# The first sequence's 47-point transform kept in its input tile and regrouped by transfers between partitions

## The chip, the cores and the metric

The kernel runs on one core of a Trainium2 chip. The metric is the device time of one execution in microseconds (us). The five engines are named as in the profile: PE (TensorE, matrix products), PEld (its weight loads), DVE (VectorE), ACT (ScalarE), POOL (GpSimd) and SP (SyncE, which here only issues transfers). SPq, ACTq and POOLq are the three queues from which transfers are issued.

## The reference

The input x holds 8 sequences of 3008 positions by 256 channels. Each sequence is transformed, mixed, shrunk and transformed back, and the result goes through a gated two-layer network.

```
X = rfft(x, axis=1)
Yr = soft(Xr @ w_r - Xi @ w_i + b_r, 0.01);  Yi = soft(Xr @ w_i + Xi @ w_r + b_i, 0.01)
y = irfft(Yr + 1j * Yi, n=3008, axis=1)
out = (sigmoid(y @ w_gate) * (y @ w_val)) @ w_out        # 256 -> 1536 -> 256
```

Here soft(v, l) = sign(v) * max(|v| - l, 0). The network's weights come in as 64-bit floats and are turned into pairs of shorter floats on the chip ("conversion").

## The kernel before

3008 = 47 * 64. The transform of a sequence runs in two steps. Step A (`fwd_a`, L176) is a 47-point transform along the partitions: 94 input partitions hold 47 positions for each half j of the 64, a table `fa_sb` has 96 columns, and the 96 outputs are 24 frequencies k by four rows (real or imaginary part, half j). A sequence has 32 columns of 256 channels; `load_a` (L165) brings four columns at a time as two transfers (64 and 30 partitions), so h runs from 0 to 7. `fwd_a` makes two products of 512 columns per h, and ACT and DVE copy the results from PSUM back over the input tile, in place. `half_a` (L192) is the same for two columns at a time and is used for the third group of sequences (called `beside`).

Step B (`fwd_b`, L226) is a 64-point transform for two frequencies at a time, so a sequence has 12 steps q. It needs the 64 positions of a frequency, real and imaginary, on 128 partitions. So the outputs of step A are regrouped: `store_a` (L183) writes them to `zd` in DRAM, and `load_b` (L221) reads `zd` back into the tile `zf` with another arrangement of partitions. For the first sequence, step q then does `fwd_b(0, q)`, `mix4(0, q-1)` (the mixing, 24 products) and `inv_b(0, q-2)` (the inverse 64-point transform, 4 products), whose result `vz` goes to `vd` in DRAM. Later `load_v` (L313) reads `vd` and `inv_a` (L329) makes the inverse 47-point transform, whose output is the network's input. `load_mf` and `load_mi` bring the tables of each step, two buffers each.

The order at the beginning is written out by hand (L827 to L896, `manual_schedule`): all loads of the first sequence; its step A with the stores on SP, and four loads of the second sequence between them; tables and biases; step A of the second sequence for h = 0 to 3 with the stores on POOL; then the loop over q = 0 to 13 with the first sequence's steps and, beside them, conversion of the first weights (`load_part`, `start_part`, `ops`); then step A of the second sequence for h = 4 to 7. Behind it the first chunk of the network runs, 12 units `ffn[f]`: `ffn1` makes 12 products of 512 columns, conversion of the next weights hangs in its gaps (`hook`), and after each unit come five or six `half_a`. What is not in a manual block is placed by the planner where an engine has room; that is how two loads of the table `mis` and their copies to `md` (L216, L217, on POOL) come to stand near the end of the loop. Before anything, `WARM` = 24 products of zeros run on PE (L817). Each engine and each queue works in the order in which it is given its instructions, so a waiting transfer holds those behind it on its queue.

The lines the change touches are the step A helpers (L146 to L197), `load_b` (L221), the fused biases (L744), `load_part` and `start_part` (L786, L795) and the manual order (L815 to L896).

Of the kernel before, what the change touches and what calls it, by code (L numbers as in the profile page):

```python
# [20 lines left out]
NK2 = 24  # L21
# [13 lines left out]
PRE = 2  # L35
WARM = 24
EARLY = 8
NCONV = 7
# [23 lines left out]


def _tables(seq):
    n2 = np.arange(R2)
    k2 = np.arange(NK2)
    c, s = _cs(n2[:, None] * k2[None, :], R2)
    fa = np.zeros((R2, 2, NK2, 2, 2))
    fb = np.zeros((NK2, 2, 2, 128))
    for j in range(2):  # L70
        fa[:, j, :, 0, j] = c
        fa[:, j, :, 1, j] = -s
        fb[:, 0, j, j:2 * R2:2] = c.T / seq
        fb[:, 1, j, j:2 * R2:2] = -s.T / seq
    fa = fa.reshape(2 * R2, 2 * NQ)
    fb = fb.reshape(2 * NQ, 128).astype(np.float32)
# [27 lines left out]
    return {"mf": mf, "mi": mi, "mis": mis, "fa": fa.astype(np.float32), "fb": fb}  # L104


@with_exitstack
def tile_fft_mix_ffn(ctx: ExitStack, tc, x, w_r, w_i, b_r, b_i, w_one, w_out, mf, mi, mis, fa, fb, out):
    nc = tc.nc
# [36 lines left out]
    fa_sb = cw.tile([2 * R2, 2 * NQ], F32, name="fa_sb")  # L146
    nc.scalar.dma_start(fa_sb, fa)

# [16 lines left out]
    def load_a(b, h):  # L165
        xf = p0.tile([P, 4, D], F32, name="xf0", bufs=R1 // 8) if b == 0 else big("xf")
        for lo_, hi_ in ((0, 64), (64, 2 * R2)):
            nc.sync.dma_start(xf[lo_:hi_], xv[b, lo_:hi_, 4 * h:4 * h + 4])
        held["x", b, h] = xf

    def product_a(xi, az, copy):
        pa = bank("pa")[:2 * NQ]
        nc.tensor.matmul(pa, fa_sb, xi, start=True, stop=True)  # L173
        copy(az, pa.rearrange("p (h c) -> p h c", h=2))  # L174

    def fwd_a(b, h):  # L176

        xf = held["x", b, h]
        for i in range(2):
            at = slice(2 * i, 2 * i + 2)  # L180
            product_a(xf[:2 * R2, at], xf[:2 * NQ, at], nc.vector.tensor_copy if b < 2 and i else nc.scalar.copy)

# [3 lines left out]
    def load_half(b, h):  # L186
        xf = p2.tile([P, 2, D], F32, tag="ld", bufs=NLD, name="xfh")
        for lo_, hi_ in ((0, 64), (64, 2 * R2)):
            nc.sync.dma_start(xf[lo_:hi_], xv[b, lo_:hi_, 2 * h:2 * h + 2])
        held["xh", b, h] = xf  # L190
# [30 lines left out]
    def load_b(b, q):  # L221
        zf = p2.tile([P, 2, D], F32, tag="ld", bufs=NLD, name="zf")
        nc.sync.dma_start(zf, zd[b][4 * q:4 * q + 4].rearrange("(q a) n c -> (a n) q c", q=2))
        held["z", b, q] = zf

    def fwd_b(b, q, m, full):  # L226
# [141 lines left out]
    def converting(place):  # L368

        if place == 0:  # L370
            ops("hi", 0)
            n = len(started)
            start_part(p2)
# [53 lines left out]

    def fft_units(bs):

        aa = [(b, h) for b in bs for h in range(R1 // 8)]  # L430
        ms = {}
        units = []
# [10 lines left out]
        def loads(q, b):  # L443
            if b == bs[0]:
                if q == 0:
                    ms[0, 0] = load_mf(0)
                if q + 1 < NP:
                    ms[q + 1, 0] = load_mf(q + 1)
                if 0 <= q - 1 < NP:
                    ms[q - 1, 1] = load_mi(q - 1, False)  # L450
# [287 lines left out]
    def load_mix():  # L738
        for w in (w_r, w_i):
            wf = f2k("wf")  # L740
            nc.sync.dma_start(wf, w.rearrange("(t p) d -> p t d", p=P))
            wfs.append(wf)

    def load_bias():  # L744
        for i, v in enumerate((b_r, b_i)):
            nc.sync.dma_start(bias_sb[:, i], v.rearrange("(o d) -> o d", o=1).broadcast_to([P, D]))
            nc.sync.dma_start(bias4[64 * i:64 * i + 64], v.rearrange("(o d) -> o d", o=1).broadcast_to([64, D]))

    def mix_weights():
        wi = p0.tile([P, CT, 2, D], F32R, tag="xf0", bufs=R1 // 8, name="wi_sb")  # L750
        nc.scalar.copy(wi[:, :, 0], wfs[1])
# [7 lines left out]
        sub(bias_sb[:, 1], bias_sb[:, 1], bias_sb[:, 0])  # L759
        return wi  # L760
# [25 lines left out]
    def load_part():  # L786
        k, f = parts.pop(0)
        if len(parts) >= 3 * NF // 2 - NCONV:
            raw = p0.tile([P, 2, D, 2], U32, tag="xf0", bufs=R1 // 8, name="raw0")
# [5 lines left out]
    def start_part(pool):  # L795
        if not raws:
            return
        k, f, raw = raws.pop(0)
        e = pool.tile([P, 2, D], U32, tag="f2k", bufs=NF2K if pool is p2 else 2, name="cv_e")
        if k:  # L800
# [17 lines left out]
    for _ in range(WARM):  # L818
        nc.tensor.matmul(warm, zero[:, :P], zero, start=True, stop=True)
    second_fft = fft_units(groups[1])[1]  # L820
    third_fft = fft_units(groups[2])[1]
    ffn, own0, u0 = ffn_units()
    na = R1 // 8
    early = EARLY // 2
    nc.vector.memset(ebias, -896.0 * 2.0 ** 23)
    mfs, mis_ = {}, {}
    with tc.manual_schedule():  # L827
        for h in range(na):
            load_a(0, h)
        load_mix()  # L830
        for h in range(na):
            fwd_a(0, h)
            store_a(0, h, nc.sync)
            if 0 <= h - 2 < early:
                load_a(1, h - 2)
        mfs[0] = load_mf(0)
        load_bias()
        for q in range(2):
            load_b(0, q)
        mfs[1] = load_mf(1)  # L840
        for h in range(early):
            fwd_a(1, h)
            store_a(1, h, nc.gpsimd)
            if h == 1:
                wi_sb = mix_weights()
        nc.sync.dma_start(fb_sb, fb)
        for _ in range(2):
            load_part()
        for q in range(NP + 2):
            if q + 2 < NP:  # L850
                load_b(0, q + 2)
            if 0 <= q - 1 < NP:
                mis_[q - 1] = load_mi(q - 1, True)
            if len(parts) > 3 * NF // 2 - NCONV and q % 2 or q == NP:
                load_part()
            if q % 2 == 0 and 4 <= q < 4 + 2 * (na - early):
                load_a(1, early + q // 2 - 2)
            if q < NP:
# [4 lines left out]
            if q % 2:  # L863
                ops("sum word", 0)
                start_part(p0)
                ops("exp low top", -1)
            elif q:
                ops("power mant", -1)
                if len(started) > 1:
                    ops("hi lo", 0)  # L870
                ops("one", -1)
            if 0 <= q - 1 < NP:
                mix4(0, q - 1)
            if 0 <= q - 2 < NP:
                inv_b(0, q - 2, mis_[q - 2], True)
        beside = [(b, h) for b in groups[2] for h in range(R1 // 4)]
        for bh in beside[:2]:
            load_half(*bh)
        left = ["hi lo", "power mant one", "sum word", "hi lo"]
        for h in range(early, na):  # L880
            fwd_a(1, h)
            store_a(1, h, nc.gpsimd)
            ops(left.pop(0), 0)
    p0s.close()
    p3 = p3s.enter_context(tc.tile_pool(name="p3", bufs=2, side="right", reuse_waits="tile"))
    with tc.manual_schedule():
        for u in own0:
            load_v(u)
        for f in range(NF):
            ffn[f]()  # L890
            for i in range(f * len(beside) // NF, (f + 1) * len(beside) // NF):
                if i + 2 < len(beside):
                    load_half(*beside[i + 2])
                half_a(*beside[i])
            if parts:
                load_part()  # L896
    hook.clear()

# [18 lines left out]

    (a3, q3), (a4, q4) = (fft_units(g) for g in groups[3:])
    n = len(a3) // 3
# [112 lines left out]
```

## Time and profile before

| what | value |
|---|---|
| median of 3 runs (lowest, highest) | 2847.21 us (2844.71, 2848.36) |
| profiled execution, its own time | 2847.25 us |
| its span | 2845.1 us |
| PE busy in the span | 2810.8 us (99%) |
| PEld, DVE, ACT, POOL busy | 2315.3, 2082.7, 1320.1, 713.6 us |
| PE busy in the first 220 us | 199.15 us, granted clock 0.95 |
| PE busy in the other 2625 us | 2611.69 us, granted clock 1.00 |
| moved by DMA in the first 220 us | 235 GB/s, engines' mean busy share 0.76 |

The span runs from the first to the last instruction of the profiled execution. A busy share is the part of a stretch in which the engine worked, and the granted clock is 1.00 at 2.4 GHz and 0.50 at 1.2 GHz.

### The profile page before, as it was taken

Reading aid. Unit: us, or ns where it says so; the run is one execution under the profiler, and the core shown is the slowest. Engines: PE = TensorE matmul, PEld = TensorE weight load, DVE = VectorE, ACT = ScalarE, POOL = GpSimd, SP = SyncE. Lnnn points to the kernel's source line nnn. Section 1 sums busy time; section 2 is a strip of 40 time slices with the busy share of each in tenths; the row PEclk is TensorE's granted clock in tenths of the full one; section 3 lists DMA queues with packets and bytes.
Section 4 is the critical chain, followed back from the end, with each engine's and each line's share of the span. In section 5 each row is a group of like instructions: output and inputs, shape, how many; then the busy total and the mean of one; then the engine's idle time right before and its main releaser. Section 6 shows DMA issues by size and latency. Waiting matters only on the chain.

```text
span 2845.1 us, 38347 instructions
## 1 busy us (share of the span) xinstructions
PE 2810.8 (99%) x13892; PEld 2315.3 (81%) x13892; DVE 2082.7 (73%) x3109; ACT 1320.1 (46%) x2294; POOL 713.6 (25%) x642
## 2 busy tenths in 40 slices
PE   8899999999999999999999999999999999999999
PEld 6668888888899987888888888888888888888887
DVE  5668778767678635777777777777777777777776
ACT  4565544555445443444444444444444444444443
POOL 0111001113300001333333333333333333333321
PEclk9999999999999999999999999999999999999999
DMA  8676645666544472000000000000000000000000
GB/s 274 199 237 191 180 136 157 182 181 198 176 144 147 155 207 69 20 11 30 30 30 16 15 30 30 18 13 30 30 30 15 16 30 31 19 11 30 30 16 15
DMA packets 174510, 240.49 MB, mean 85 GB/s; under 512 B 15793, under 2 KB 126097, under 8 KB 174321
## 3 DMA queue, kind: packets, MB, share of 16 engines
q1 hardware_dynamic: 164368, 212.84, 24.4%
q0 software_dynamic: 9856, 25.17, 2.7%
q8 instruction: 110, 1.80, 0.3%
q14 instruction: 80, 0.65, 0.1%
q10 hardware_dynamic: 96, 0.04, 0.0%
HBM read 133.65 MB, written 104.33 MB: 84 GB/s over the span
## 4 chain that ended last, share of the span: by engine, by line
PE 91%; DMA 3%; DVE 3%; issue 2%; ACT 1%; SPq 0%; POOL 0%; DVEq 0%; POOLq 0%; ACTq 0%
PE pd L645 11%; PE pc L645 11%; PE pa L645 11%; PE po L622 8%; PE po L621 8%; PE po L620 7%; PE pm L265 5%; PE pb L645 5%; PE pia L334 4%; PE pb L231 3%; PE pa L173 2%; PE pg L390 2%; PE pg L392 2%; PE pg L391 2%; PE po L415 2%; PE po L416 2%
## 5 line engine op out<-in xcount | busy, mean ns | idle before, releaser
L622 PE MATMUL po<-hl,w 128*128 128x512 f32 x912 | 362.9, 398 | 0.0
L621 PE MATMUL po<-hh,w 128*128 128x512 f32 x912 | 362.0, 397 | 0.0
L620 PE MATMUL po<-hh,w 128*128 128x512 f32 x912 | 361.0, 396 | 0.0
L704 POOL TENSOR_TENSOR c<-c,c 128x512 f32<-128x512 f32 x114 | 147.4, 1293 | 834.5 <-DVE c L700 633.5
L645 PE MATMUL pc<-s,w1h 128*128 128x512 f32 x912 | 284.2, 393 | 1.4 <-DVE v L679 1.4
L645 PE MATMUL pa<-a,w1h 128*128 128x512 f32 x912 | 284.2, 393 | 0.0
L700 DVE TENSOR_TENSOR c<-u,pc 128x512 f32<-128x512 f32 x228 | 156.7, 687 | 115.7 <-PE pc L645 107.4
L675 DVE TENSOR_TENSOR u<-u,pb 128x512 f32<-128x512 f32 x228 | 155.3, 681 | 91.0 <-PE pb L645 64.7
L592 ACT CAST hh<-v 128x512 fp32r<-128x512 f32 x114 | 70.7, 620 | 305.6 <-DVE v L685 305.6
L622 PEld LDWEIGHTS po<-hl,w 128*128 128x128 f32 x912 | 171.6, 188 | 41.8
L620 PEld LDWEIGHTS po<-hh,w 128*128 128x128 f32 x912 | 172.2, 189 | 40.8
L621 PEld LDWEIGHTS po<-hh,w 128*128 128x128 f32 x912 | 171.2, 188 | 40.5
L645 PEld LDWEIGHTS pa<-a,w1h 128*128 128x128 f32 x912 | 171.3, 188 | 40.0
L645 PEld LDWEIGHTS pc<-s,w1h 128*128 128x128 f32 x912 | 171.0, 188 | 39.5 <-DVE v L679 2.3
L596 POOL TENSOR_TENSOR hl<-c,hh 128x512 fp32r<-128x512 f32 x114 | 152.5, 1338 | 186.2 <-ACT hh L592 186.2
L265 PE MATMUL pm<-w_sb,xsh 128*128 128x256 f32 x1008 | 190.4, 289 | 1.5 <-ACT xf L174 1.1
L645 PE MATMUL pc<-s,w1l 128*128 128x512 f32 x456 | 177.7, 390 | 0.0
L645 PE MATMUL pa<-a,w1l 128*128 128x512 f32 x456 | 177.1, 388 | 0.0
L677 DVE TENSOR_TENSOR v<-u,pd 128x512 f32<-128x512 f32 x228 | 156.8, 688 | 24.6 <-PE pd L645 0.6
L706 DVE TENSOR_TENSOR u<-u,pd 128x512 f32<-128x512 f32 x228 | 156.9, 688 | 24.4 <-DVE c L700 0.9
L679 DVE TENSOR_TENSOR v<-v,pc 128x512 f32<-128x512 f32 x228 | 156.6, 687 | 24.4 <-DVE v L677 0.9
L671 ACT COPY u<-pa 128x512 f32<-128x512 f32 x228 | 133.7, 586 | 81.8 <-PE pa L645 81.8
(165 smaller groups left out, 6769.7 us busy)
## 6 DMA issues: line engine op xcount, KB each, us to landing
zf<-zd SPq DMA_DIRECT2D x96, 256.0 KB, 3.5
vf<-vd SPq DMA_DIRECT2D x128, 192.0 KB, 3.2
out_dram<-ot SPq DMA_DIRECT2D x93, 256.0 KB, 2.2
vd<-vz SPq DMA_DIRECT2D x84, 256.0 KB, 2.8
ypair<-yd SPq DMA_DIRECT2D x19, 1024.0 KB, 4.9
yd<-yf SPq DMA_DIRECT2D x103, 188.0 KB, 2.9
zd<-xf SPq DMA_DIRECT2D x40, 384.0 KB, 3.4
xf<-in_x_dram SPq DMA_DIRECT2D x48, 256.0 KB, 4.3
```

What stands on the lines that cost most here:

```text
L265: nc.tensor.matmul(o, l, r, start=(i == 0), stop=(i == len(mms) - 1))
L596: sub_(hl, h, hh)
L620: nc.tensor.matmul(o, wh, hh, start=(f == 0), stop=False)
L621: nc.tensor.matmul(o, wl, hh, start=False, stop=False)
L622: nc.tensor.matmul(o, wh, hl, start=False, stop=(f == NF - 1))
L645: nc.tensor.matmul(o, l, r, start=not more and l is wh and r is xh, stop=l is wl, skip_group_check=more)
L675: add(u, u, b)
L677: add(v, u, d)
L679: add(v, v, c)
L700: add(c12, u, c)
L704: nc.gpsimd.tensor_mul(c12, g12, c12)
L706: add(u, u, d)
```

## The change

The first sequence gets a single tile `xz` of 32 columns instead of eight tiles. Its step A uses a table `fa0` whose columns stand in another order, so that frequency k's four output rows lie at partitions `_row(k)`, +4, +8 and +12. They are not stored to DRAM. `load_b0(q)` builds `zf` by eight transfers within the chip, each from one partition of `xz` (32 KB in a row) to 32 partitions of `zf` (1 KB each): four on SP for the step's first frequency, four on POOL for the second. `store_a` and `load_b` stay for the other sequences.

Around it the order changes. `WARM` is 13. Two h of the second sequence's step A (not four) come before the loop; h = 2 and 3 run in the loop at q = 2 and 4, ahead of `fwd_b`, h = 4 at q = 13 ahead of the last `inv_b`, and h = 5 to 7 after the loop. The stores of h = 0 to 3 go from POOL to SP. The biases for the first sequence are loaded by `load_bias4` before the loop, the other biases and `fb_sb` at q = 3. Weight parts are loaded at even q into three buffers of their own. The tiles of `half_a` come from `r2k` (four buffers) instead of `ld` (three). Three `half_a` run before the first unit of the network, and the next weight part is loaded right behind them. The two `mis` tables are loaded by hand at f = 2 and 3.

```diff
-WARM = 24
-EARLY = 8
+WARM = 13
+EARLY = 2
+AT_FIRST = 3
...
+def _row(k):
+    return k // 8 * 32 + k % 2 * 16 + k % 8 // 2
...
+    for k in range(NK2):
+        fa0[:, _row(k):_row(k) + 16:4] = fa[:, 4 * k:4 * k + 4]
...
+    xz = p0.tile([P, R1 // 2, D], F32, name="xz")
...
     def load_a(b, h):
-        xf = p0.tile([P, 4, D], F32, name="xf0", bufs=R1 // 8) if b == 0 else big("xf")
+        xf = big("xf") if b else xz[:, 4 * h:4 * h + 4]
...
     def load_half(b, h):
-        xf = p2.tile([P, 2, D], F32, tag="ld", bufs=NLD, name="xfh")
+        xf = r2k("xfh").bitcast(F32)
...
+    def load_b0(q):
+        zf = p2.tile([P, 2, D], F32, tag="ld", bufs=NLD, name="zf")
+        for w in range(4):
+            for i in range(2):
+                at = _row(2 * q + i) + 4 * w
+                (nc.gpsimd if i else nc.sync).dma_start(zf[32 * w:32 * w + 32, i], xz[at:at + 1])
+        held["z", 0, q] = zf
...
     with tc.manual_schedule():
         for h in range(na):
             load_a(0, h)
+        nc.sync.dma_start(fa_sb, fa)
+        load_a(1, 0)
         load_mix()
+        load_a(1, 1)
         for h in range(na):
             fwd_a(0, h)
-            store_a(0, h, nc.sync)
-            if 0 <= h - 2 < early:
-                load_a(1, h - 2)
         mfs[0] = load_mf(0)
-        load_bias()
         for q in range(2):
-            load_b(0, q)
+            load_b0(q)
+        load_bias4()
         mfs[1] = load_mf(1)
-        for h in range(early):
+        for h in range(EARLY):
             fwd_a(1, h)
-            store_a(1, h, nc.gpsimd)
-            if h == 1:
+            load_a(1, EARLY + h)
+            if h == 0:
                 wi_sb = mix_weights()
-        nc.sync.dma_start(fb_sb, fb)
-        for _ in range(2):
-            load_part()
         for q in range(NP + 2):
             if q + 2 < NP:
-                load_b(0, q + 2)
+                load_b0(q + 2)
             if 0 <= q - 1 < NP:
                 mis_[q - 1] = load_mi(q - 1, True)
-            if len(parts) > 3 * NF // 2 - NCONV and q % 2 or q == NP:
+            if q < EARLY:
+                store_a(1, q)
+            elif q < 4 + EARLY and q % 2 == 0:
+                h = EARLY + q // 2 - 1
+                fwd_a(1, h)
+                store_a(1, h)
+            if q == 3:
+                nc.sync.dma_start(fb_sb, fb)
+                load_bias()
+            if q % 2 == 0 and q <= NP:
                 load_part()
...
+            if q == NP + 1:
+                fwd_a(1, 2 * EARLY)
+                store_a(1, 2 * EARLY, nc.gpsimd)
             if 0 <= q - 2 < NP:
                 inv_b(0, q - 2, mis_[q - 2], True)
-        for bh in beside[:2]:
+        for bh in beside[:NR2K]:
             load_half(*bh)
...
         for u in own0:
             load_v(u)
+        halves(AT_FIRST)
+        load_part()
         for f in range(NF):
             ffn[f]()
-            for i in range(f * len(beside) // NF, (f + 1) * len(beside) // NF):
-                if i + 2 < len(beside):
-                    load_half(*beside[i + 2])
-                half_a(*beside[i])
             if parts:
                 load_part()
+            if f in (2, 3):
+                tables[f - 2, 1] = load_mi(f - 2, False)
+            halves(AT_FIRST + (f + 1) * (len(beside) - AT_FIRST) // NF)
```

`halves(n)` runs `half_a` up to the n-th and issues, behind each, the load that is four further on.

## Rows read from the trace of the kernel before

**Rows 1.** Windows: stretch, length, busy us (instructions) of PE PEld DVE ACT POOL, clock, DMA, GB/s

```profile
220.00:2845.00 2625.00, 2611.69 (x12954) 2171.02 (x12952) 1947.54 (x2878) 1197.68 (x2074) 681.25 (x582) 1.00 0.23 72
```

**Rows 2.** Waits of PE, first 220 us: us in total, times, longest

```profile
PE pb L231 <- DMA zf<-zd: 7.0, 1, 7.0
PE pia L334 <- DMA vf<-vd: 4.5, 1, 4.5
PE pa L173 <- ACT cv_e L770: 2.6, 1, 2.6
...
PE pb L231 <- DMA mf_sb<-in_mf_dram: 1.3, 1, 1.3
PE pi L299 <- ACT vz L306: 1.2, 1, 1.2
PE pa L173 <- DMA xf<-in_x_dram: 1.0, 3, 0.5
```

**Rows 3.** PE in order of time: start, us, engine, line, operation, shape, count

```profile
1.46 7.10 PE L819 MATMUL warm<-zero 128*128 128x512 f32 x24 [1.46 <-DVE ebias L825]
...
38.13 3.76 PE L231 MATMUL pb<-mf_sb,zf 128*128 128x128 f32 x16 [6.99 <-DMA zf<-zd]
...
50.71 1.05 PE L231 MATMUL pb<-mf_sb,zf 128*128 128x128 f32 x8
...
98.05 7.56 PE L173 MATMUL pa<-xf,fa_sb 94*96 94x512 f32 x16
...
110.07 5.34 PE L334 MATMUL pia<-fb_sb,vf 96*128 96x94 f32 x24 [4.46 <-DMA vf<-vd]
...
117.39 0.63 PE L390 MATMUL pg<-yth,w1h 128*128 128x512 f32 x1
117.81 0.63 PE L391 MATMUL pg<-ytl,w1h 128*128 128x512 f32 x1
...
123.03 0.39 PE L392 MATMUL pg<-yth,w1l 128*128 128x512 f32 x1
123.26 0.39 PE L390 MATMUL pg<-yth,w1h 128*128 128x512 f32 x1
```

**Rows 4.** Windows of the first loads, of step B's begin, of the loop, and of 110 to 120

```profile
4.00:16.00 12.00, 12.00 (x37) 6.35 (x37) 2.43 (x4) 3.61 (x5) 0.00 (x0) 1.00 1.03 248
38.00:42.00 4.00, 3.87 (x18) 3.90 (x19) 0.72 (x2) 1.44 (x4) 0.96 (x2) 0.52 1.04 404
...
50.00:92.00 42.00, 42.00 (x330) 40.98 (x328) 37.16 (x64) 29.49 (x55) 6.48 (x9) 1.00 0.80 239
...
110.00:120.00 10.00, 9.45 (x34) 8.29 (x35) 3.00 (x6) 4.96 (x9) 0.00 (x0) 0.51 0.30 102
```

**Rows 5.** Transfers by issue: count, KB each, us to landing; 0 to 1.2, 300 to 900, 30 to 33

```profile
xf<-in_x_dram SPq DMA_DIRECT2D x1, 256.0 KB, 3.6
...
zf<-zd SPq DMA_DIRECT2D x64, 256.0 KB, 3.3
...
mf_sb<-in_mf_dram SPq DMA_DIRECT2D x32, 128.0 KB, 2.5
...
zf<-zd SPq DMA_DIRECT2D x2, 256.0 KB, 7.5
```

**Rows 6.** SP's queue in order of time: start, us of issuing, transfer, count

```profile
0.74 9.57 SPq L168 DMA_DIRECT2D xf<-in_x_dram  x16
...
104.80 10.95 SPq L317 DMA_DIRECT2D vf<-vd  x4
```

**Rows 7.** DVE in order of time, the last two copies of step A

```profile
20.77 0.69 DVE L174 COPY xf<-pa 96x512 f32<-96x512 f32 x1 [1.03 <-PE pa L173]
22.49 0.69 DVE L174 COPY xf<-pa 96x512 f32<-96x512 f32 x1 [1.03 <-PE pa L173]
```

**Rows 8.** POOL in order of time, around the last result of the loop

```profile
100.92 0.71 POOL L217 DMA_DIRECT2D md<-mi_sb  x1 [1.69 <-DMA mi_sb<-in_mis_dram]
101.63 0.72 POOL L307 DMA_DIRECT2D vd<-vz  x1
```

More of the change, by code (lines that the diff above doesn't have):

```diff
@@ L75, in _tables @@
     fa = fa.reshape(2 * R2, 2 * NQ)
+    fa0 = np.zeros_like(fa)
+    for k in range(NK2):
+        fa0[:, _row(k):_row(k) + 16:4] = fa[:, 4 * k:4 * k + 4]
+    fa0 = fa0.astype(np.float32)
     fb = fb.reshape(2 * NQ, 128).astype(np.float32)
@@ L103, in _tables, with tile_fft_mix_ffn @@
         mis[q, :, 0], mis[q, :, 1] = _split(e.reshape(128, 128))
-    return {"mf": mf, "mi": mi, "mis": mis, "fa": fa.astype(np.float32), "fb": fb}
+    return {"mf": mf, "mi": mi, "mis": mis, "fa0": fa0, "fa": fa.astype(np.float32), "fb": fb}
 @with_exitstack
-def tile_fft_mix_ffn(ctx: ExitStack, tc, x, w_r, w_i, b_r, b_i, w_one, w_out, mf, mi, mis, fa, fb, out):
+def tile_fft_mix_ffn(ctx: ExitStack, tc, x, w_r, w_i, b_r, b_i, w_one, w_out, mf, mi, mis, fa0, fa, fb, out):
     nc = tc.nc
@@ L146, in tile_fft_mix_ffn @@
     fa_sb = cw.tile([2 * R2, 2 * NQ], F32, name="fa_sb")
-    nc.scalar.dma_start(fa_sb, fa)
+    fa0_sb = p0.tile([2 * R2, 2 * NQ], F32, name="fa0_sb")
+    nc.scalar.dma_start(fa0_sb, fa0)
+    xz = p0.tile([P, R1 // 2, D], F32, name="xz")
     zd = [tc.dram_tile([NQ, R1, D], F32, name=f"zd{b}") for b in range(B)]
@@ L169, in load_a, with product_a @@
         held["x", b, h] = xf
-    def product_a(xi, az, copy):
+    def product_a(xi, az, copy, table=fa_sb):
         pa = bank("pa")[:2 * NQ]
-        nc.tensor.matmul(pa, fa_sb, xi, start=True, stop=True)
+        nc.tensor.matmul(pa, table, xi, start=True, stop=True)
         copy(az, pa.rearrange("p (h c) -> p h c", h=2))
@@ L180, in fwd_a @@
             at = slice(2 * i, 2 * i + 2)
-            product_a(xf[:2 * R2, at], xf[:2 * NQ, at], nc.vector.tensor_copy if b < 2 and i else nc.scalar.copy)
+            product_a(xf[:2 * R2, at], xf[:2 * NQ, at], nc.vector.tensor_copy if b < 2 and i else nc.scalar.copy,
+                      fa_sb if b else fa0_sb)
     def store_a(b, h, queue=nc.sync):
@@ L372, in converting @@
             n = len(started)
-            start_part(p2)
+            start_part()
             if len(started) > n:
@@ L425, in ffn2, with fft_units @@
                 nc.sync.dma_start(out[ct * P:(ct + 1) * P, c * CW:(c + 1) * CW], ot)
-    def fft_units(bs):
+    def fft_units(bs, ms):
         aa = [(b, h) for b in bs for h in range(R1 // 8)]
-        ms = {}
         units = []
@@ L448, in loads @@
                     ms[q + 1, 0] = load_mf(q + 1)
-                if 0 <= q - 1 < NP:
+                if 0 <= q - 1 < NP and (q - 1, 1) not in ms:
                     ms[q - 1, 1] = load_mi(q - 1, False)
@@ L742, in load_mix, with load_bias4 @@
             wfs.append(wf)
+    def load_bias4():
+        for i, v in enumerate((b_r, b_i)):
+            nc.sync.dma_start(bias4[64 * i:64 * i + 64], v.rearrange("(o d) -> o d", o=1).broadcast_to([64, D]))
     def load_bias():
@@ L746, in load_bias @@
             nc.sync.dma_start(bias_sb[:, i], v.rearrange("(o d) -> o d", o=1).broadcast_to([P, D]))
-            nc.sync.dma_start(bias4[64 * i:64 * i + 64], v.rearrange("(o d) -> o d", o=1).broadcast_to([64, D]))
     def mix_weights():
-        wi = p0.tile([P, CT, 2, D], F32R, tag="xf0", bufs=R1 // 8, name="wi_sb")
+        wi = p0.tile([P, CT, 2, D], F32R, name="wi_sb")
         nc.scalar.copy(wi[:, :, 0], wfs[1])
@@ L758, in mix_weights @@
             sub(w_sb[:, :, 1, i], w, w_sb[:, :, 0, i])
-        sub(bias_sb[:, 1], bias_sb[:, 1], bias_sb[:, 0])
         return wi
@@ L788, in load_part @@
         if len(parts) >= 3 * NF // 2 - NCONV:
-            raw = p0.tile([P, 2, D, 2], U32, tag="xf0", bufs=R1 // 8, name="raw0")
+            raw = p0.tile([P, 2, D, 2], U32, name="raw0", bufs=3)
         else:
@@ L793, in load_part, with start_part @@
         raws.append((k, f, raw))
-    def start_part(pool):
+    def start_part():
         if not raws:
@@ L798, in start_part @@
         k, f, raw = raws.pop(0)
-        e = pool.tile([P, 2, D], U32, tag="f2k", bufs=NF2K if pool is p2 else 2, name="cv_e")
+        e = p2.tile([P, 2, D], U32, tag="f2k", bufs=NF2K, name="cv_e")
         if k:
@@ L819, in tile_fft_mix_ffn, with halves @@
         nc.tensor.matmul(warm, zero[:, :P], zero, start=True, stop=True)
-    second_fft = fft_units(groups[1])[1]
-    third_fft = fft_units(groups[2])[1]
+    tables = {}
+    second_fft = fft_units(groups[1], tables)[1]
+    third_fft = fft_units(groups[2], {})[1]
     ffn, own0, u0 = ffn_units()
     na = R1 // 8
-    early = EARLY // 2
     nc.vector.memset(ebias, -896.0 * 2.0 ** 23)
     mfs, mis_ = {}, {}
+    beside = [(b, h) for b in groups[2] for h in range(R1 // 4)]
+    waiting = list(beside)
+    def halves(upto):
+        while waiting:
+            i = len(beside) - len(waiting)
+            if i >= upto:
+                break
+            half_a(*waiting.pop(0))
+            if i + NR2K < len(beside):
+                load_half(*beside[i + NR2K])
     with tc.manual_schedule():
@@ L829, in tile_fft_mix_ffn @@
             load_a(0, h)
+        nc.sync.dma_start(fa_sb, fa)
+        load_a(1, 0)
         load_mix()
+        load_a(1, 1)
         for h in range(na):
             fwd_a(0, h)
-            store_a(0, h, nc.sync)
-            if 0 <= h - 2 < early:
-                load_a(1, h - 2)
         mfs[0] = load_mf(0)
-        load_bias()
         for q in range(2):
-            load_b(0, q)
+            load_b0(q)
+        load_bias4()
         mfs[1] = load_mf(1)
-        for h in range(early):
+        for h in range(EARLY):
             fwd_a(1, h)
-            store_a(1, h, nc.gpsimd)
-            if h == 1:
+            load_a(1, EARLY + h)
+            if h == 0:
                 wi_sb = mix_weights()
-        nc.sync.dma_start(fb_sb, fb)
-        for _ in range(2):
-            load_part()
         for q in range(NP + 2):
             if q + 2 < NP:
-                load_b(0, q + 2)
+                load_b0(q + 2)
             if 0 <= q - 1 < NP:
                 mis_[q - 1] = load_mi(q - 1, True)
-            if len(parts) > 3 * NF // 2 - NCONV and q % 2 or q == NP:
+            if q < EARLY:
[8 more added lines that the diff above has]
+            if q % 2 == 0 and q <= NP:
                 load_part()
-            if q % 2 == 0 and 4 <= q < 4 + 2 * (na - early):
-                load_a(1, early + q // 2 - 2)
+            if q % 2 == 0 and 4 <= q < 4 + 2 * (na - 2 * EARLY):
+                load_a(1, 2 * EARLY + q // 2 - 2)
             if q < NP:
@@ L864, in tile_fft_mix_ffn @@
                 ops("sum word", 0)
-                start_part(p0)
+                start_part()
                 ops("exp low top", -1)
@@ L871, in tile_fft_mix_ffn @@
                 ops("one", -1)
+            if q == 4:
+                sub(bias_sb[:, 1], bias_sb[:, 1], bias_sb[:, 0])
             if 0 <= q - 1 < NP:
                 mix4(0, q - 1)
+            if q == NP + 1:
+                fwd_a(1, 2 * EARLY)
+                store_a(1, 2 * EARLY, nc.gpsimd)
             if 0 <= q - 2 < NP:
                 inv_b(0, q - 2, mis_[q - 2], True)
-        beside = [(b, h) for b in groups[2] for h in range(R1 // 4)]
-        for bh in beside[:2]:
+        for bh in beside[:NR2K]:
             load_half(*bh)
         left = ["hi lo", "power mant one", "sum word", "hi lo"]
-        for h in range(early, na):
+        for h in range(2 * EARLY + 1, na):
+            ops(left.pop(0), 0)
             fwd_a(1, h)
             store_a(1, h, nc.gpsimd)
-            ops(left.pop(0), 0)
+        ops(left.pop(0), 0)
     p0s.close()
@@ L916, in merge @@
                                          enumerate(streams) for i, u in enumerate(s)), key=lambda t: t[:2])]
-    (a3, q3), (a4, q4) = (fft_units(g) for g in groups[3:])
+    (a3, q3), (a4, q4) = (fft_units(g, {}) for g in groups[3:])
     n = len(a3) // 3
```

## The prediction

> **What bounds the kernel now.** I read the windows first, because the change touches only the beginning. From 220 us on PE is busy 2611.69 of 2625 us at clock 1.00 [rows 1]: that part is bound by PE, its work stays as it is, and what the beginning wins or loses should reach the end in full. In the first 220 us the list of PE's waits is the next view [rows 2]. It names where PE stood: 7.0 us for the regrouped tile zf, 4.5 for vf (the result read back from DRAM), 2.6 for a conversion on ACT, 1.3 for a table mf, 1.2 for vz, 1.0 for the second sequence's x. Third comes PE in order of time [rows 3]: it shows stretches at half the clock behind two of the waits. The 16 products from 38.13 take 3.76 us where eight take 1.05 later. From 110.07 the 24 inverse products take 5.34, and the network's products follow each other every 0.42 us (117.39, 117.81) against 0.23 (123.03, 123.26). The granted clock was 0.52 from 38 to 42 and 0.51 from 110 to 120 [rows 4], behind 7.0 and 4.5 us in which PE had nothing to do. So the stakes are some 18 us of waits, about 8 us of slow clock, and the zeros at the start.
>
> **The change part by part**, against the profiled execution's own 2847.25 us (span 2845.1), which is the median of the runs (2847.21) but for 0.04.
>
> *Zeros.* Eleven of 24 go. They are the last and ran at the full clock: 11 x 0.23 = 2.5 us. PE is then ready near 6.0. The first x transfer lands 0.74 + 3.6 = 4.3 [rows 5, 6], its second half about 0.6 later, so the data is there. Later h come every 385 KB / 248 GB/s = 1.55 us [rows 4] and are used every 1.72 [rows 7], so no wait follows. **-2.5**; nothing if x came at 8.4.
>
> *Second sequence's x.* Its three waits (1.0) fall on h = 1 to 3, of which two now run in the loop, 10 us after their load. **-1.0.**
>
> *The regrouping.* The last copy of step A ended at 22.49 + 0.69 = 23.2 [rows 7], so now at 20.7. DRAM's round trip from there to 38.13 was 15 us. Now SP issues four transfers and POOL four beside it. SP's x loads took 9.57 / 16 = 0.6 us each to issue [rows 6], POOL's 0.7 [rows 8]; at 0.6 the fourth goes out at 22.5. How long 32 KB from one partition takes, no row shows. From below, at 404 GB/s [rows 4], it is 0.1 us behind the landing time; from above, if the rate goes by partitions, the loads to 94 partitions give 248 / 94 = 2.6 GB/s and 12 us. I take the landing of an undisturbed zf, 3.3 us [rows 5], because a set of eight moves the same 256 KB into the same tile: 25.8. PE finishes its four early products at 23.1 (20 products of 0.86 from 6.0) and waits 2.7.
>
> Behind these four, SP issues the next four, two biases and only then mf(1): seven more of 0.6, so it leaves at 26.7 and lands 2.5 later [rows 5], at 29.2. PE has done the first fwd_b by 26.7 and waits 2.5 again. mf(2) stands behind four x loads, four transfers of the next set, a store and a weight part, leaves near 32.7 and lands at 35.2. PE meanwhile has fwd_b(1) (0.9), mix4(0) (2.8, a step of 4.6 less 0.9 each for fwd_b and inv_b) and the moved step A of h = 2 (1.7), to 34.7: 0.5 left of the 1.3 before. In all 5.7 for 8.3; issues at 0.4 would make it 4. I take **-3.0**, with bounds -6 and +3 (a landing of 7.5, as zf had at 30 us [rows 5]). The slow products at 38.13 cost 3.76 - 2 x 1.05 = 1.6; as PE's waits are now split I keep half: **-0.8**.
>
> *The loop.* A step is 36 instructions; 330 in 42 us [rows 4] make 9.2 steps, 4.6 us each, with PE full. The moved products of the second sequence are the same work elsewhere, cost nothing, and at q = 13 they fill the 1.2 us wait for vz: **-1.2**. Per step SP now issues four transfers, mf, mi and on average one more, 7 x 0.6 = 4.2 us of 4.6; POOL four and vd, 3.5. Both queues just keep up. zf has three buffers, so a set is issued over two steps ahead (9 us): this cover hides a slow landing, though not a low rate. On SP, store_a(1, 2) waits for its copies, with a weight part and mf(4) behind it; mf is needed a step later. The 3 MB that zd took each way on DRAM are gone, and the engines' share in the loop was 0.80. For the extra waits at each fwd_b I put **+1.0** (bounds 0 and the slower rival).
>
> *From the last product to vf.* Before: the last inverse products ended near 98.05, vd was issued at 101.63 behind the copy to md, which waited 1.69 us for its table [rows 8], vf left at 104.80 [rows 6], and PE began at 110.07 [rows 3]: 12.0 us, with 7.6 of step A as cover. Of the 3.6 us between the products and vd's issue, vz's copy (as DVE's, 0.7) and its start need about 0.9. The tables have moved to f = 2 and 3, and ACT's conversion is done under the step A put in front, so up to 2.7 go: 9.3. Cover: three h (5.1) and three half_a (2.6), 7.7. Left: 1.6 of 4.5, and the half_a were due anyway. **-3.0**, bounds 0 and -4.5. The table's copy on POOL now stands among the half_a stores; a unit's 18 products of 0.23, 4.1 us, cover it.
>
> *Clock behind it.* Full clock would halve the 5.34 us of inverse products (-2.7) and save ten products 0.19 each (-1.9). After a wait of 1.6 us I expect it to hold, less what copies between them take: **-4.0**, bounds 0 and -4.6.
>
> *The weight part.* The conversion in the network's second unit waited for a part that SP issues behind half loads, which wait for buffers; ACT stood still, and PE 2.6 us [rows 2]. Its products then ran slow again, some seven at 0.19 more (1.4). Now the next part is issued ahead of the first unit and the one after it ahead of the unit's half loads. **-3.0**, bounds 0 and -4.0.
>
> Sum: -2.5 - 1.0 - 3.0 - 0.8 - 1.2 + 1.0 - 3.0 - 4.0 - 3.0 = -17.5, so 2847.25 - 17.5 = 2829.8, say **2830 us**.
>
> **The rivals.** *Slower: the loop becomes bound by the transfers.* Each of the eight reads a single partition. In the rows the narrower loads (64 and 30 partitions) kept the DMA engines full at 248 GB/s, the wider ones at 404 [rows 4], so narrowness costs. If a queue's four went one after another, each as long as the shortest landing read (2.5 [rows 5]), a step would take 10 us in place of 4.6: ten steps lose 54, less the 17.5: 2884. It decides from 4.6 / 4 = 1.15 us per transfer and queue. Against it: 16 x loads issued 0.6 apart were in flight together, and the sets lie 9 us ahead.
>
> The Trainium skill speaks for this rival ("SBUF — State Buffer", Door 1: the DMA port swizzle): four neighbouring partitions share a port of about 27 GB/s. An estimate from that page is 1.2 us per transfer, right at the deciding point with two queues side by side; a set's eight rows lie on eight ports. "DMA: Bandwidth & Descriptors" (Issuing engines are not separate DMA queues) adds that both queues use the same 16 engines; with no overlap at all the estimate is 9.7 us a step. The 248 against 404 GB/s agree in direction; no row here shows one partition.
>
> *No change: the waits come back.* If the sets land in 7.5 us, as zf did, fwd_b starts at 30.0 after 6.9 us without work, the clock falls again, mf(2) and vf are as late as before, and the slow stretch at 110 stays. Left are the zeros, x and vz: -4.7, so 2842.5, or up to 2848 with the loop's +1 and a late weight part. The half clock behind both long waits speaks for it, DRAM's vanished traffic against it.
>
> *More: everything at its bound*, -27: 2820.
>
> **How the numbers follow.** Forecast 0.64, its own range 2821 to 2840; everything 0.06; no change 0.15; slower 0.15. About 0.2% (5.7 us) is what a measurement of this kernel can tell from no change: faster is below 2841.5, slower above 2852.9. The forecast and the larger gain (0.70) and a little of the no-change case (0.02) are faster, 0.72; 0.13 same; 0.15 slower. The range of 8 in 10 starts at 2820 and takes in no change and the loop's small losses, to 2856; a loop at 10 us a step is left out.
>
> **What would show it.** Right: PE's first x product near 6; fwd_b near 26; waits for zf and mf of about 2.5 each; loop steps of 4.6; no half clock after vf; no wait for conversion at the second unit. Wrong: loop steps above 5 us with PE waiting for zf, or clock 0.5 after vf again.

## The result and the profile after

The median went from 2846.04 us (2841.47 to 2849.46, 17 runs) to 2852.64 us (2847.74 to 2857.38, 17 runs): a ratio of 1.0021, 95% interval 1.0015 to 1.0027. The change makes the kernel 6.6 us slower, where 17 us less were forecast. The profiled execution took 2857.38 us (span 2855.5), the slowest of its 17, so some 4.7 us of what its rows lose are its own; that of the kernel before (2847.25) lies 1.2 above its median.

First the first 220 us of the kernel before, then two windows of the kernel after (columns as in [rows 1]):

```profile
0.00:220.00 220.00, 199.15 (x940) 144.23 (x941) 135.12 (x232) 122.41 (x220) 32.31 (x60) 0.95 0.76 235
```

```profile
0.00:220.00 220.00, 192.88 (x862) 139.49 (x863) 126.42 (x216) 117.44 (x212) 54.87 (x104) 0.91 0.77 215
220.00:2855.00 2635.00, 2622.59 (x13021) 2178.52 (x13019) 1958.13 (x2893) 1203.43 (x2083) 678.33 (x582) 1.00 0.24 72
```

Behind 220 us PE stands for 12.4 us; before it was 13.3 [rows 1]. So, as assumed, nothing changed there but that 10.9 us of PE's work came in late. The loss is in the first 220 us: 862 products done where it was 940 (11 of the missing ones are zeros), at clock 0.91 and not 0.95. PE's waits there, against [rows 2]:

```profile
PE pa L187 <- ACT carry L370: 5.0, 1, 5.0
PE pb L255 <- DMA zf<-xz: 3.8, 2, 2.3
PE pb L255 <- DVE ys L313: 3.0, 1, 3.0
PE pb L255 <- DVE yc L279: 3.0, 1, 3.0
PE pa L187 <- ACT azh L188: 2.8, 2, 2.3
PE pb L255 <- DMA xf<-in_x_dram: 2.5, 1, 2.5
...
PE pia L358 <- DMA vf<-vd: 1.3, 1, 1.3
```

The 7.0 us for zf and the 4.5 for vf have shrunk, the 2.6 for conversion and 1.2 for vz are gone, and waits that the kernel before did not have stand in their place. PE in order of time says where (the counterpart of [rows 3]):

```profile
6.13 14.06 PE L187 MATMUL pa<-xz,fa_sb 94*96 94x512 f32 x32
...
26.21 2.05 PE L255 MATMUL pb<-mf_sb,zf 128*128 128x128 f32 x8 [1.50 <-DMA zf<-xz]
30.75 2.05 PE L255 MATMUL pb<-mf_sb,zf 128*128 128x128 f32 x8 [2.49 <-DMA xf<-in_x_dram]
...
41.70 1.43 PE L255 MATMUL pb<-mf_sb,zf 128*128 128x128 f32 x8 [3.03 <-DVE ys L313]
...
66.59 2.05 PE L255 MATMUL pb<-mf_sb,zf 128*128 128x128 f32 x8 [2.98 <-DVE yc L279]
...
88.97 1.13 PE L255 MATMUL pb<-mf_sb,zf 128*128 128x128 f32 x8 [2.27 <-DMA zf<-xz]
...
95.16 1.05 PE L255 MATMUL pb<-mf_sb,zf 128*128 128x128 f32 x8
...
117.50 3.67 PE L358 MATMUL pia<-fb_sb,vf 96*128 96x94 f32 x16 [1.33 <-DMA vf<-vd]
...
197.35 2.02 PE L187 MATMUL pa<-xfh,fa_sb 94*96 94x512 f32 x2 [5.01 <-ACT carry L370]
```

Until 31 us all goes as forecast: step A at 6.13, the first `fwd_b` at 26.21 and not 38.13 [rows 3]. The wait of 2.49 us is the forecast one for mf(1), which SP issued at 27.41; the profile names the x load behind it. Then the lead of 12 us, of which 3.4 are the two h moved into the loop, melts. The last of the twelve `fwd_b` starts at 95.16; in the kernel before it started at 87.49:

```profile
87.49 1.05 PE L231 MATMUL pb<-mf_sb,zf 128*128 128x128 f32 x8
```

Eight products take 2.05 or 1.43 us behind four of the five waits in step B, 1.13 behind the fifth, and 1.05 elsewhere. The granted clock was 0.50 from 30.7 to 35.0 and from 66.5 to 69.5, 0.61 from 41.7 to 45.0 and 0.64 from 88.9 to 93.5. From the first to the last `fwd_b` pass 69.0 us. At full clock and without waits the products between them need some 49 us, an estimate from the steps of 4.6 (the first two are short by `mix4` and `inv_b`) and two h of 1.72. The four waits inside are 10.8 us, so some 9 us are slow clock.

The two waits for DVE lead back to SP's queue. Lists of SP and of DVE of the kernel after, around 56 to 65 us:

```profile
56.64 0.42 SPq L818 DMA_DIRECT2D raw<-in_w_one_dram  x1
57.12 3.32 SPq L182 DMA_DIRECT2D xf<-in_x_dram  x2
60.54 0.39 SPq L217 DMA_DIRECT2D mf_sb<-in_mf_dram  x1
61.10 2.44 SPq L247 DMA_DIRECT2D zf<-xz  x4
64.42 0.38 SPq L224 DMA_DIRECT2D mi_sb<-in_mi_dram  x1
```

```profile
64.38 0.43 DVE L795 TENSOR_SCALAR cv_e<-raw 128x512 uint32<-128x512 uint32 x1 [1.80 <-DMA raw<-in_w_one_dram]
64.72 0.69 DVE L313 TENSOR_TENSOR ys<-pm,bias 128x512 f32<-128x512 f32 x1
```

The weight part left at 56.64 and landed 7.7 us later; DVE stood for it with the mixing's result queued behind. SP has hardly a gap until 90.5 us: adding up its rows from 26 to 95 us gives 58.3 us of issuing for 89 transfers (short gaps inside a row included), more than the 49 us of products beside them.

### The profile page after: what moved, and what is told of

Read it like the earlier page. It is cut to its first block, busy times and chain, and to the rows that moved or that the text cites. A ratio compares the mean times of both kernels' runs of the same rounds, so it can differ in the third digit from the quotient of the medians.

```text
span 2855.5 us, 38477 instructions
## 1 busy us (share of the span) xinstructions
PE 2815.5 (99%) x13881; PEld 2318.0 (81%) x13881; DVE 2084.5 (73%) x3109; ACT 1320.9 (46%) x2294; POOL 733.2 (26%) x686
## 4 chain that ended last, share of the span: by engine, by line
PE 92%; DVE 3%; DMA 2%; issue 1%; ACT 1%; SPq 0%; POOL 0%; DVEq 0%; ACTq 0%; POOLq 0%
PE pd L669 11%; PE pc L669 11%; PE pa L669 11%; PE po L646 8%; PE po L645 7%; PE po L644 7%; PE pm L289 5%; PE pb L669 5%; PE pia L358 4%; PE pb L255 3%; PE pa L187 3%; PE pg L414 2%; PE pg L416 2%; PE po L439 2%; PE pg L415 2%; PE po L440 2%
```

## The experiments

Theory A, from the rows above: the start gains what was forecast, and the edits beside it lose it again, by SP's full queue, the parts' shorter lead, the tables' copies and f = 9. Rival B: the transfers within the chip are themselves the loss. Ratios are against the kernel before, with 95% intervals. It was timed again beside each group of runs, with medians from 2844.12 to 2846.04 us, so a difference between medians of two groups is uncertain by some 2 us. Each kernel starts from the changed one unless it says otherwise.

### The side edits, one by one

**The weight parts one step earlier.**

```diff
+        load_part()                # ahead of the loop, into another tile
         for q in range(NP + 2):
...
-            if q % 2 == 0 and q <= NP:
-                load_part()        # now behind the step's conversion
```

> Theory A (the weight part has lost its lead): the changed kernel loads a part at even q and starts its conversion one step later; DVE and ACT stand in order behind it, and PE's two waits of 3.0 us at 38 and 63 us and the slow clock behind them are its price. One part loaded ahead of the loop gives the lead back: both waits go, -6 to -9 us against the changed kernel's 2852.6, so 2844 to 2847 (ratio to the kernel before 0.999 to 1.000). Theory B (the single-partition transfers are slow, and what is late is zf): nothing changes, 2851 to 2854 (1.002).

2849.77 us, 1.0018 (1.0010 to 1.0027), between the two theories' ranges and not told from the changed kernel (1.0015 to 1.0027). The two waits of 3.0 us for DVE went, but zf now has three waits (4.1 us), one `fwd_b` stands 3.1 us for none that the profile names, and mi 1.6. Theory A falls as put: the late part was the first of several late transfers.

**The copies of the tables later.**

```diff
-                nc.gpsimd.dma_start(m, t.bitcast(F32))
+                later.append(lambda: nc.gpsimd.dma_start(m, t.bitcast(F32)))
...
+            if f in (5, 6):
+                later.pop(0)()
```

> The copies of the two mis tables to md are issued three units later than their loads. Theory A (on POOL the copy waits 6.4 to 7.7 us for its table, the stores of half_a stand behind it, ACT waits for their buffers and PE for ACT): PE's waits of 0.5, 2.3 and 1.2 us between 154 and 167 us go, -3 to -5, so 2848 to 2850 (1.0005 to 1.001). Theory B (the engines are full of transfers and the stores would land late anyway): 2852 to 2853 (1.002).

2848.68 us, 1.0015 (1.0006 to 1.0023), in theory A's range, though the interval overlaps that of the changed kernel. The 2.8 us of azh waits ahead of step A's products are gone from its rows. They came from POOL, which held its stores behind each copy for the table's landing (kernel after):

```profile
147.25 0.72 POOL L232 DMA_DIRECT2D md<-mi_sb  x1 [7.71 <-DMA mi_sb<-in_mis_dram]
147.97 1.56 POOL L212 DMA_DIRECT2D zd<-azh  x3
```

**Two half_a at f = 9.**

```diff
-            halves(AT_FIRST + (f + 1) * (len(beside) - AT_FIRST) // NF)
+            halves(AT_FIRST + (2, 4, 7, 9, 12, 14, 16, 19, 22, 24, 26, 29)[f])
```

> Only the number of half_a behind each unit is changed: two instead of three behind the unit f = 9, one more behind f = 8. Theory A (that unit has an inverse product too; with three half_a it needs four PSUM banks of three, and the fourth waits until ACT has copied the carry): PE's wait of 5.0 us at 192 and some 2 us of slow clock go, -5 to -7, so 2846 to 2848 (1.000 to 1.0005). Theory B (ACT and DVE are behind PE in these units, the wait only moves on): 2851 to 2853 (1.0015 to 1.0025).

2844.11 us, 0.9998 (0.9989 to 1.0006). One `half_a` moved from f = 9 to f = 8 gives back 8.5 us by medians of two groups. Against the kernel before it is 6.9 us (0.3 less where the changed kernel took 6.6 more), as theory A said: the wait of 5.0 goes and the network's products behind it, which followed each other every 0.43 us from 199.6 to 202.6, are back at 0.23.

**mf(1) and the x loads ahead of the first sets.**

```diff
         mfs[0] = load_mf(0)
+        mfs[1] = load_mf(1)
+        load_bias4()
+        for h in range(EARLY):
+            load_a(1, EARLY + h)
         for q in range(2):
             load_b0(q)
-        load_bias4()
-        mfs[1] = load_mf(1)
...
-            load_a(1, EARLY + h)
```

> SP issues mf(1), the biases and the second sequence's x for h = 2 and 3 before the first two regrouped sets, in the time in which it waits for step A anyway. Theory A (mf(1) is late because ten issues of 0.6 us stand ahead of it): PE's wait of 2.5 us at 28 goes, the sets for q = 2 and 3 leave 3.5 us earlier, -2 to -5, so 2848 to 2851 (1.0005 to 1.0015). Theory B (x and tables compete with the sets for the engines): the first zf wait grows by what the second loses, 2852 to 2854 (1.002).

2856.03 us, 1.0035 (1.0022 to 1.0048), above both ranges. In its rows it is theory B: SP's first set now leaves behind the x loads, the first wait for zf grows from 1.5 to 5.0 us while the second is gone, and a later wait grows to 6.3 us. On a queue without a gap, one transfer's lead is another's delay.

### Who is slow in the loop

**Parts, mi and early biases on POOL.**

```diff
-        nc.sync.dma_start(raw...)    # also mi_sb and bias4; parts at the head of their step
+        nc.gpsimd.dma_start(raw...)
```

> The loop's weight parts, its mi tables and the two early biases are issued on POOL, the parts at the head of their step; all else as changed. Theory A (SP's queue is what fell behind: it issues without a gap from 21 to 94 us, and the 3.0 us waits at 41.7 and 66.6, the 2.3 at 89 and the 2.5 at 30.8 are its late transfers): the first two waits go, mf(1) leaves 1.2 us earlier, the slow clock behind them goes with them, 5 to 8 us less than the changed kernel, 2845 to 2848. Rival B (transfers within the chip hold up everything that is in flight beside them, whoever issues it): the parts land as late as before, 2851 to 2854.

2851.69 us, 1.0019 (1.0010 to 1.0028), rival B's number: A falls here too. POOL's list shows a reason other than rival B's, a transfer that waits for one with which it shares no tile:

```profile
27.11 0.52 POOL L770 DMA_DIRECT2D bias<-in_b_i_dram  x1
27.61 0.57 POOL L818 DMA_DIRECT2D raw<-in_w_one_dram  x1
28.17 2.96 POOL L247 DMA_DIRECT2D zf<-xz  x6
31.36 0.50 POOL L247 DMA_DIRECT2D zf<-xz  x1 [0.23 <-DMA bias<-in_b_i_dram]
37.07 0.50 POOL L247 DMA_DIRECT2D zf<-xz  x1 [5.22 <-DMA raw<-in_w_one_dram]
```

The transfer at 31.36 is the eighth behind the bias and waits for it to land; the one at 37.07 is the eighth behind the part and waits 5.22 us. On SP in the fence further up, mi at 64.42 is the eighth behind the part, and the list of waits has 0.8 us for it there:

```profile
SPq L224 <- DMA raw<-in_w_one_dram: 0.8, 1, 0.8
```

In these rows a queue never has more than eight transfers under way.

**The order alone: the first sequence through zd.**

```diff
+            store_a(0, h)       # fa0 in fa's order
...
-            load_b0(q)          # and load_b0(q + 2) in the loop
+            load_b(0, q)
```

> The changed kernel's order and all its side edits, but the first sequence goes through zd in DRAM again. Theory A (the regrouping on chip is itself a gain of about 10 us at the start of step B, its queue load a loss of some 6 in the loop): first fwd_b near 36 us, 2855 to 2862. Rival B (the transfers between partitions are the loss): 2840 to 2847.

2844.20 us, 0.9998 (0.9989 to 1.0006), 8.4 us under the changed kernel. Rival B's number: the regrouping on chip is the loss, though it starts step B 7 us earlier. Step B's first and last `fwd_b` in this kernel:

```profile
33.29 2.04 PE L255 MATMUL pb<-mf_sb,zf 128*128 128x128 f32 x8 [8.28 <-DMA zf<-zd]
...
88.91 1.05 PE L255 MATMUL pb<-mf_sb,zf 128*128 128x128 f32 x8
```

55.6 us here, 69.0 with the regrouping (26.21 to 95.16). More than half of SP's waits here (26 to 95 us) are for a buffer that PE frees, so SP is ahead of PE:

```profile
SPq L224 <- PE pi L323: 17.2, 10, 3.3
```

**The other two edits together.** Both diffs above, then with the POOL queue.

> Two half_a at f = 9 and the copies of the mis tables at f = 5 and 6, together. If the two losses stand apart (the carry wait at f = 9 with its slow clock, the azh waits at f = 5 and 6): -7 and -3 add up, 2840 to 2842, faster than the kernel before. If what the tables held up is made good by the time of f = 9: as with f = 9 alone, 2843.5 to 2845.

> The two edits of the kernel just above and the POOL queue for parts, mi tables and early biases. Theory A: 5 to 8 us below that kernel, 2833 to 2837. Rival B: no gain by the queue, 2840 to 2842.

2842.08 us, 0.9990 (0.9981 to 0.9999), and 2841.87 us, 0.9989 (0.9980 to 0.9998). The two losses add up, about 10 us, as expected; moving transfers to POOL's queue again brings nothing that can be told.

### What in the regrouping costs

**Neighbouring partitions.**

```diff
-                at = _row(2 * q + i) + 4 * w
+                at = 4 * (2 * q + i) + w     # fa0 in fa's order
```

> The changed kernel, but a set's eight rows lie on eight neighbouring partitions (SP's four on four neighbours, POOL's on the next four) and not on _row's places, 4 apart and 16 apart. Theory P (neighbours share a way out of the tile, and that is what a set pays for): SP's four go through one such way, a set takes about four times as long, the loop's steps grow past 4.6 us, 2865 to 2890. Theory E (a 1 KB packet from a single partition holds its DMA engine some 2.5 times as long as one from DRAM, 0.62 busy at 78 GB/s from 21.5 to 25.5 us against 1.01 at 319 before, wherever the partition is): as the changed kernel, 2850 to 2855.

2890.27 us, 1.0154 (1.0140 to 1.0168), the end of theory P's range. It holds for neighbours: 37.6 us more, with landings of 5.1 and 6.4 us (SP, POOL) where the changed kernel has 3.9 and 3.3. These are the loads of zf from 21 to 100 us in this kernel (name, queue, count, KB, median us to landing):

```profile
zf<-xz SPq DMA_DIRECT2D x36, 32.0 KB, 5.1
zf<-xz POOLq DMA_DIRECT2D x36, 32.0 KB, 6.4
```

The Trainium skill ("SBUF — State Buffer", Door 1: the DMA port swizzle), by which four neighbouring partitions share a port, agrees with this.

**Eight small transfers from DRAM.** The order alone, with zf read in eight pieces.

```diff
-                load_b(0, q)
+                for w in range(4):
+                    for i in range(2):
+                        at = 4 * (2 * q + i) + w
+                        (nc.gpsimd if i else nc.sync).dma_start(zf[32 * w:32 * w + 32, i], zv[0][at])
```

> The changed order with the first sequence through zd in DRAM, but zf is read back by eight transfers of 32 KB, four on SP and four on POOL as in the changed kernel, where the kernel that took 2844.2 read it by one of 256 KB. Theory S (many small transfers and their issues are the loss): 2850 to 2854, as the changed kernel. Theory P (a single partition as the source is the loss): 2842 to 2846, the loop's waits for zf, mf and the weight parts absent.

2855.28 us, 1.0038 (1.0026 to 1.0051), 11.1 more than one transfer of 256 KB and just above theory S's range. With no single partition as a source, it is as slow as the regrouping on chip. SP's waits in this kernel (26 to 95 us) are mostly for landings of others, but for the 4.7 us for the stores that it reads back, and mi's longest is again the eighth behind the part:

```profile
SPq L247 <- DMA zd<-xz: 4.7, 3, 2.9
SPq L224 <- DMA raw<-in_w_one_dram: 3.9, 2, 2.9
SPq L217 <- DMA xf<-in_x_dram: 2.1, 3, 0.7
SPq L217 <- DMA raw<-in_w_one_dram: 1.3, 1, 1.3
...
SPq L774 <- DMA raw<-in_w_out_dram: 1.1, 1, 1.1
```

**Consecutive sets on other partitions.**

```diff
-    return k // 8 * 32 + k % 2 * 16 + k % 8 // 2
+    return k // 2 % 3 * 32 + k % 2 * 16 + k // 6
```

> The changed kernel with another _row: the sets of three consecutive steps lie in three different blocks of 32 partitions, so that they share no group of four; within a set the rows stay 4 and 16 apart. If sets in flight together hold each other up: the first fwd_b 0.5 to 1 us earlier, fewer of the loop's waits, 3 to 8 us less than the changed kernel, 2844 to 2849. If a single set pays the price by itself: 2850 to 2854.

> The other _row with two half_a at f = 9 and the table copies at f = 5 and 6. If sets hold each other up: 3 to 8 us below 2842.1 (the same kernel with the first _row), 2834 to 2839. If not: 2841 to 2843.

2852.62 us, 1.0030 (1.0018 to 1.0041), and with the two edits 2842.40 us, 0.9991 (0.9983 to 1.0000): no gain over the first `_row` (2852.64 and 2842.08). With a set's rows 4 apart, other blocks for consecutive sets bring nothing.

**Eight more transfers without use.** The order alone, and beside each set eight tiny transfers into a spare tile.

```diff
+                (nc.gpsimd if i else nc.sync).dma_start(spare[32 * w:32 * w + N, i], mf[0][32 * w:32 * w + N, 0:16])
```

> The changed order with the first sequence through zd (2844.2), and beside each set eight more transfers, four on SP and four on POOL, of 32 packets of 64 bytes (2 KB in all) into a tile that nobody reads. If the number of transfers and issues costs: 2850 to 2856, as with the eight real ones from DRAM (2855.3). If the bytes' time on the engines does: 2844 to 2847.

> The same with one packet of 64 bytes in each of the eight more transfers. If issuing costs: as with 32 packets, 2850 to 2856. If the packets cost: 2844 to 2847 here, and 2850 or more with 32.

2854.79 us, 1.0042 (1.0028 to 1.0055), with N = 32, and 2853.49 us, 1.0030 (1.0018 to 1.0041), with N = 1. Eight transfers of 64 bytes per set cost 9.3 us: it is their number, neither bytes nor packets. PE's waits for mf, which SP issues, grow to 8.6 and 3.7 us from 0.9 with the order alone. In the latter, SP's sets of four, 1.2 us as a rule, took 3.67 where the fourth was the eighth behind a part (wait of 2.4 us):

```profile
60.93 0.41 SPq L825 DMA_DIRECT2D raw<-in_w_one_dram  x1
61.64 1.26 SPq L182 DMA_DIRECT2D xf<-in_x_dram  x2
63.00 0.38 SPq L217 DMA_DIRECT2D mf_sb<-in_mf_dram  x1
63.43 0.47 SPq L238 DMA_DIRECT2D zf<-zd  x1
63.94 3.67 SPq L246 DMA_DIRECT2D spare<-in_mf_dram  x4
```

Part of the price may be waits for the spare tile itself (7.5 us on POOL from 20 to 100 us, 0.3 on SP).

### The best order

**The order alone with the two edits**, and **the same with the first two sets on chip**, from neighbouring rows and from rows 4 apart (there mf(1) also leaves ahead of two biases):

```diff
             load_b0(q)              # q = 0 and 1 only
...
-                load_b0(q + 2)
+                load_b(0, q + 2)
```

> The changed order with the first sequence through zd in DRAM, two half_a at f = 9, and the copies of the tables at f = 5 and 6. If the f = 9 edit gains here what it gained with the regrouping on chip (6 to 8 us; the carry wait of 5.0 is the same in both), 2836 to 2839, faster than before by 7 to 9. If the gain of f = 9 hung on the late loop: 2841 to 2844.

> The kernel just above, but the first two sets (q = 0 and 1) are regrouped on chip, from neighbouring partitions; the other ten go through zd. If the price of a set is engine time that only the full loop can't spare, and the gain is the earlier start: first fwd_b near 27 us and not 33, -3 to -6 against the kernel above, 2831 to 2835. If the eight stores of 384 KB that fill the DMA engines until 28 us hold the sixteen transfers up: first fwd_b at 30 or later, -2 to +1.

> The kernel that took 2834.5 (changed order, first sequence through zd, two half_a at f = 9, table copies at f = 5 and 6), but the first two sets are regrouped on chip from rows that lie 4 partitions apart, the other 80 rows going through zd by 12 stores of 3 or 2 h. If the port is what delayed the earlier mixture (POOL's transfers landed in 10.8 us there): first fwd_b at 27 to 28 us, -3 to -6 against 2834.5, 2828 to 2832. If the stores beside them are: first fwd_b near 32 or later, 2834 to 2842.

The first is the fastest of all: 2834.49 us, 0.9965 (0.9951 to 0.9978), faster than both kernels and below the 2836 expected. The mixtures take 2844.96 us, 0.9996 (0.9987 to 1.0005), a miss, with a wait of 13.4 us for the neighbours' sets, and 2836.84 us, 0.9976 (0.9967 to 0.9985), the time of the second expectation without its late start. First and last `fwd_b`, the fastest kernel and then the better mixture:

```profile
32.76 2.05 PE L260 MATMUL pb<-mf_sb,zf 128*128 128x128 f32 x8 [7.94 <-DMA zf<-zd]
...
87.99 1.05 PE L260 MATMUL pb<-mf_sb,zf 128*128 128x128 f32 x8
```

```profile
29.07 2.04 PE L262 MATMUL pb<-mf_sb,zf 128*128 128x128 f32 x8 [3.52 <-DMA zf<-xz]
...
88.34 1.05 PE L262 MATMUL pb<-mf_sb,zf 128*128 128x128 f32 x8
```

A start 3.7 us earlier ends 0.35 us later: the lead is lost again to waits for mf (2.2) and ys (3.1).

**The kernel before with 13 zeros.**

```diff
-WARM = 24
+WARM = 13
```

> The kernel before with 13 products of zeros in place of 24, nothing else. If step A then starts at 6.0 us and the rest moves with it: 2.5 us less, 2842 to 2844. If the first stretch is set by the transfers to and from zd (the DMA engines are full, 1.01, from 20 to 30 us) and not by PE: the 2.5 us go into a longer wait for zf, 2844.5 to 2846.

2842.61 us, 0.9990 (0.9981 to 0.9999): 3.1 less, the first theory's size. Its profile does not show that way: step A starts at 6.91, but the first `fwd_b` stands at 39.21 and the last at 87.59, no earlier than before. Where the 3.1 us were won stays open.

## Why the prediction was wrong

**The loop, +1.0, is the step that failed.** It said that both queues just keep up, with SP 4.2 us of 4.6 busy, and that sets issued 9 us ahead hide a slow landing. SP did not keep up: its 89 transfers took 58.3 us to issue beside some 49 us of products. The steps did stay at 4.6 us where no wait fell in, and the rival with transfers one after another (2884) did not come: in the changed kernel their landing was 3.9 and 3.3 us. But the reserve was counted in zf's buffers alone. On a queue without slack whatever else it carries comes late too, above all the weight parts, which took 3.8 to 7.7 us to land. Three waits of 3.03, 2.98 and 2.27 us (8.3) with slow clock behind them stand where 1.0 stood.

The count of transfers as the cause is shown by three kernels of 2853 to 2855 against 2844.2. How the count costs is read from rows, and no run parts the two ways. In the changed kernel SP's waits for landings are only 3.8 us (26 to 95 us), which points to the issuing there. But with parts, mi and biases moved to POOL, SP waits 10.2 us and POOL 10.3 us for landings, and nothing is gained. In the kernels with eight transfers from DRAM and with eight tiny ones, waits for landings, without those for the stores read back, are 11.6, 9.8 (32 packets) and 15.2 us (one packet), against 1.7 with the order alone: there the limit of eight has a large part. No run raised the limit. That zd's DRAM traffic goes was counted as relief; it bought nothing that a median shows.

**The regrouping, -3.0, was right and did not last.** The waits are 1.50 and 2.49 for 8.3, so -4.3. The start came as computed (26.21 for 25.8), but the end of the loop hangs on all its data and not on its first set.

**Zeros, vz and vd to vf were right.** -2.5 was -3.1 when tried alone, though that kernel's rows show no earlier step B, so its size is confirmed and its way is not. In the changed kernel step A did start near 6 us. vz's wait is gone; vf's is 1.33 for 4.5 (forecast 1.6). Of the second sequence's x, 0.9 of 1.0 stayed.

**Slow clock at the start of step B, -0.8, and behind vf, -4.0: neither came.** The first two `fwd_b` take 2.05 each, and the granted clock from 26 to 60 us is 0.81. Behind vf 8 inverse products ran at full clock and 16 took 3.67, together 4.7 for 5.34, and the network's products again follow every 0.43 us (granted clock 0.53 from 117 to 127; the gain is 0.6). I expected a wait of 1.6 us not to cost the clock; one of 1.33 did.

**The weight part, -3.0, moved.** Its wait at the second unit is gone. I had costed the shift of the `half_a` as "due anyway" and did not follow it to f = 9, where three now stand in place of two: 5.0 us and slow clock. This is the second failed term, and the largest that one line mends (some 7 us). The tables' copy on POOL, which I held covered by 4.1 us of products, waits 7.71 us (2.8 of it reaches PE).

By medians: the order alone is at 2844.2, as before; on-chip regrouping adds 8.4. The order's own two faults cost about 10, as the same two edits show with the regrouping (10.5) and without (9.7). Mended, the order gives 11 us; the regrouping was the part to leave out.

One sum of the prediction is wrong: the terms at their bounds make 25.4 us and not 27. And that 2852.6 lies in the range of 8 in 10 (2820 to 2856) is luck: none of the named cases had the start won and then lost again.

## What to carry to other kernels

Count transfers and not bytes: before one is split into eight, add up the time that each queue needs to issue a step's transfers, and compare the longest landing with the time in which the next eight come due. An early first tile brings nothing where the loop's end is set by the rest of its data. Price a wait with the slow clock behind it: here 10.8 us of waits brought some 9 of slow clock. When work is spread anew over units, look at each unit for the one that gets one more.

## What the runs showed of the hardware

The 16 inverse products behind a wait of 1.26 to 1.63 us for vf took 3.67 us (kernel after, 1.33), 2.82 (order alone, 1.26) and 2.00 (fastest kernel, 1.63): the length of a wait alone does not say whether the clock stays. The lines of the latter two kernels:

```profile
111.25 2.82 PE L358 MATMUL pia<-fb_sb,vf 96*128 96x94 f32 x16 [1.26 <-DMA vf<-vd]
```

```profile
110.64 2.00 PE L363 MATMUL pia<-fb_sb,vf 96*128 96x94 f32 x16 [1.63 <-DMA vf<-vd]
```

SP needed 0.60 us to issue a 32 KB transfer from the tile (four in 2.41 us) and 0.45 from DRAM (1.79, eight small transfers from DRAM), POOL 0.49 for either (1.97).
